# Token stage in 64-row parts on column tiles, W products summed by the back product, odd keys reversed by copy, and a new order

## The chip, the core and the metric

The kernel runs on one core of a Trainium2 chip. A core has engines that work side by side and meet by semaphores: TensorE (PE: matmuls; its weight loads are listed as PEld), VectorE (DVE), ScalarE (ACT) and GpSimd (POOL). SyncE (SP) issues nearly all transfers to 16 DMA engines. The metric is device time in microseconds of one execution; the profile's span runs from the first to the last instruction of one profiled execution.

## The reference

x has 2048 tokens of D = 640 features; there are 32 heads of 20 features and four segments of 512 tokens.

```python
x = A_x
g = sigmoid((x * gate_w).sum(-1))
a = _A_ref(x, wq, wk, wv, wo, beta)     # attention with memory
b = _B_ref(x, w_r, w_i)                 # spectral filter
return g * a + (1 - g) * b

# A, per segment s: q, k, v = x @ wq, x @ wk, x @ wv
logits = q @ k.T * scale + mask         # causal inside the segment
a_dot = softmax(logits) @ v
a_mem = (phi(q) @ M) / (phi(q) @ z + 1e-6)      # phi(t) = t + 1 if t > 0 else exp(t)
o = sigmoid(beta) * a_mem + (1 - sigmoid(beta)) * a_dot
M, z = M + phi(k).T @ v, z + phi(k).sum()
a = o @ wo

# B
X = rfft2(x)                            # over 2048 tokens and 640 features
b = irfft2(X * (w_r + 1j * w_i)).astype(bfloat16)
```

## The kernel before

**Order.** The program records operations with what they read and write (`Sched.op`), then `schedule` takes a list of numbers, `ORDER`, that fixes for each engine which operation comes when, and on which engine an operation with a choice runs. The wait instructions follow from the reads and writes (`emit`). A PSUM bank is given out by `place` inside `schedule`: banks 0 to 3 in one piece for scores, banks 4 to 7 one by one for the rest. Every engine works its list strictly in order; SP's list is the order in which transfers are issued.

**Attention.** `proj_tile` makes q and k transposed (features on partitions, 512 tokens as columns) with x transposed (xT) streaming; keys of every second 128-token tile are taken with their two 64-token halves swapped (`token_order`). ACT or DVE copies the result to `qu`, it goes to DRAM (`qk_scr`) and comes back as padded heads (`qkp`, 20 of 32 rows used). `qk_unit` forms scores in three kinds of units (whole 512-column pieces, 128-row pieces, and a last kind for two head groups at once), ACT takes the exponential of a whole unit (L1265) into `ex`, and POOL zeroes what the causal mask forbids (`mask`, L1286, 7 instructions per group of 4 heads). `pv_flipped` (segments 0 to 2) and `pv_group` (segment 3) multiply by the values `va`; the sums go to `ub` and to DRAM (`u_scr`). `v_part` projects the values; tiles with swapped halves are made by two 64-wide matmuls that stand side by side in PE's columns. `mem_update` and `mem_read` hold the memory.

**Spectral part (`fft`).** The tokens are split as 128 x 16. First `fold` forms sums and differences over features on DVE and POOL (L902, L907). F1 is the transform over the 128 (`fcat`). Then come 16 groups g, each of 128 rows: D (`big`,`Ac`) transforms the features, one product for the cosines and one for the sines, with 641 columns each in three matmuls; the results are copied to `Bt`. T (`Bt`,`tt`) finishes the tokens: two matmuls of 321 columns, over the cosine and over the sine part, for each of the real and imaginary outputs. W_mul (L1441) multiplies each with w_r and w_i at once into `Pt`; two W_add (L1446, on DVE or POOL) form real and imaginary part `Yt`. The back product Tb (`tt`,`Yt`) makes three chunks of 256 columns from both parts, and its copy goes to `Cp`. After all groups, Db (`big`,`Cp`) transforms the features back (16 steps, two types, three chunks of 128, 128 and 65 rows), and L1487 sums the halves into `G`.

**End.** `finish_tile` adds, in one PSUM bank, the gated spectral rows (`G`,`fbg`) and the projection with wo (`wo`,`oU`, L513, split by 32 columns; for segment 3 `wo`,`oTl`), copies to `ot` and writes out.

In the profile almost all matmuls have the line of the helper `mms`, L515 (L513 where a matmul is split by 32 columns), and copies from PSUM those of `copy_alts`, L524 (ACT) and L526 (DVE); so go by the names.

Of the kernel before, what the change touches and what calls it, by code (L numbers as in the profile page):

```python
# [20 lines left out]
VW = 22  # L21

# [22 lines left out]
class Op:  # L45
    __slots__ = ("id", "alts", "preds", "succs", "prio", "banks", "nbytes", "npred", "eng", "t0", "t1",
                 "stamp", "need_inc", "dyn", "first", "outside", "name", "dma", "key", "xfer", "lock", "mode", "emode", "hold", "width")


class Sched:  # L50
    HOP = 70.0
# [8 lines left out]
    def op(self, alts, r=(), w=(), prio=0.0, nbytes=0, name="", after=(), dma=False, xfer=0.0, lock=False, mode=0, hold=False, width=16):  # L60
# [24 lines left out]
        for b in w2:  # L85
            bb = b
            if isinstance(b, Bank):
                o.banks.append(b)
                b.ops.append(o)
                bb = b.buf  # L90
            dep(bb.w)
            for q in bb.r:
                dep(q)
# [10 lines left out]
        if name in ("gate_tab", "den_gate") and not o.banks:  # L104
# [4 lines left out]
    COST = {(0, 1): 94.0, (0, 2): 94.0, (1, 0): 110.0, (1, 2): 110.0, (2, 0): 110.0, (2, 1): 94.0,  # L109
            (0, 4): 105.0, (1, 4): 105.0, (2, 4): 105.0, (4, 0): 105.0, (4, 1): 105.0, (4, 2): 105.0}  # L110

    def schedule(self, pools, order, nsem=56):


        ops = self.ops
        queue = {e: [] for e in self.eng}
        for v in order:
            o = ops[v // 2]
            o.eng = list(o.alts)[v % 2]
            queue[o.eng].append(o)  # L120
        for o in ops:
            o.dyn, o.t1 = [], None
            o.first = [b for b in o.banks if b.ops[0] is o]
            for b in o.banks:
                b.left = len(b.ops)
        pe, held = queue["pe"], {}
        for i, o in enumerate(pe):
            o.emode = o.mode
            if o.mode < 0:
                modes = [held[id(b)] for b in o.banks if id(b) in held]  # L130
                if not modes and i and pe[i - 1].emode not in (1, 4):
                    modes = [pe[i - 1].emode]
                for q in pe[i + 1:] if not modes else ():
                    m = q.mode if q.mode >= 0 else held.get(id(q.banks[0]), -1)
                    if m >= 0:
                        modes = [0 if m == 1 else m]
                        break
                o.emode = (modes + [0])[0]
            if o.emode not in (1, 4):
                for b in o.banks:  # L140
                    held[id(b)] = o.emode
        pos = {e: 0 for e in self.eng}
        free = {e: 0.0 for e in self.eng}
        port = mode = 0
        level = {k: {q: 0.0 for q in v} for k, v in pools.items()}
        users = {}
        ring = [0.0] * 16
        sems = [[0.0, i, None] for i in range(nsem)]
        issued = []
        self.order = []  # L150

        def place(b, lev):
            best = None
            for pool in b.pools:
                v = lev[pool]
                for q in v:
                    run = [v.get(q + i) for i in range(b.n)]
                    if None not in run and (best is None or max(run) < best[0] - 1e-9):
                        best = (max(run), pool, q)
            return best  # L160

        def window():
            tot, i = 0, len(issued) - 1
            while i >= 0 and tot <= self.WINDOW:
                tot += issued[i].nbytes
                i -= 1
            return issued[i] if i >= 0 else None

        def head(e):
            if pos[e] == len(queue[e]):  # L170
                return None
            o = queue[e][pos[e]]
            t = free[e]
            for p in o.preds:
                if p.t1 is None:
                    return None
                if p.eng != "pe" or e != "pe":
                    t = max(t, p.t1 + self.HOP)
            if o.first:
                lev = {k: dict(v) for k, v in level.items()}  # L180
                for b in o.first:
                    got = place(b, lev)
                    if got is None:
                        return None
                    t = max(t, got[0])
                    for i in range(b.n):
                        lev[got[1]][got[2] + i] = None
            if o.dma:
                gate = window()
                if gate is not None:  # L190
                    t = max(t, gate.t1 + self.HOP)
            if e == "dve" and o.lock:
                t = max(t, free["pool"])
            elif e == "pool":
                t = max(t, port)
            return t

        while len(self.order) < len(order):
            best = None
            for e in self.eng:  # L200
                t = head(e)
                if t is not None and (best is None or t < best[0] - 1e-9):
                    best = (t, e)
            if best is None:
                raise RuntimeError("order cannot be kept: " + str([(e, queue[e][pos[e]].name, queue[e][pos[e]].id) for e in self.eng if pos[e] < len(queue[e])]))
            t, e = best
            o = queue[e][pos[e]]
            pos[e] += 1
            for b in o.first:
                _, b.pool, b.bank = place(b, level)  # L210
                for q in range(b.bank, b.bank + b.n):
                    level[b.pool][q] = None
                    o.dyn.extend(users.get(q, ()))
            o.t0 = t
            occ, lat = o.alts[e][1:]
            if e == "pe" and o.emode != mode:
                occ += self.COST[mode, o.emode]
                mode = o.emode
            free[e] = o.t1 = t + occ
            if e == "dve" and o.lock:  # L220
                port = t + occ
            if o.dma:
                if o.hold:
                    free[e] = max(free[e], max(ring) + 170.0)
                for q in range(o.width):
                    ring[q] = max(ring[q], free[e] + 1300.0) + o.xfer
                o.t1 = max(ring[:o.width])
                free[e] += 43.0
                gate = window()
                if gate is not None:  # L230
                    o.dyn.append(gate)
                issued.append(o)
                sems.sort(key=lambda q: (q[0], q[1]))
                sm = sems[0]
                if sm[2] is not None:
                    o.dyn.append(sm[2])
                sm[0], sm[2] = o.t1, o
                o.stamp = sm[1]
            o.t1 += lat
            self.order.append(o)  # L240
            for b in o.banks:
                b.left -= 1
                if b.left == 0:
                    for q in range(b.bank, b.bank + b.n):
                        users[q] = list(b.ops)
                        level[b.pool][q] = max(p.t1 for p in b.ops) + self.HOP
        self.makespan = max(o.t1 for o in ops)
# [215 lines left out]
class Kern:  # L463
# [342 lines left out]
    def record(self):  # L806
# [4 lines left out]
        for s in range(NSEG):  # L811
            self.project(s)
            if s > 0:
                self.mem_read(s)
# [794 lines left out]
```

## Time and profile before

| | us |
|---|---|
| Median of three runs (range) | 242.41 (241.71 to 244.06) |
| Span of the profiled execution | 239.9 |
| ACT exponentials L1265, 92 instructions | 138.7 |
| POOL masks L1286, 224 instructions | 121.3 |
| DVE W_mul L1441, 32 x 0.822 | 25.6 |
| W_add L1446, 16 on POOL, 16 on DVE | 11.7 and 5.5 |

The profile gives for each group of like instructions the summed busy time, the mean of one and the idle time ahead of them on their engine with what ended it. Instructions of one engine can overlap at their edges, so busy time counts the union. A matmul's time includes a tail in which the next one already streams; the distance from start to start is the better price. The DMA engines moved 42.1 MB; their mean busy share is above 0.9 in several slices of the first third. The granted TensorE clock is 1.00 throughout.

### The profile page before, as it was taken

What the parts mean: (1) busy time and instruction counts of PE and PEld (TensorE: products, weight loads), DVE (VectorE), ACT (ScalarE), POOL (GpSimd) and SP (SyncE); (2) the same over time, 40 slices, a digit from 0 to 9 for tenths busy, and PEclk for the clock granted to TensorE, in tenths of its full rate; (3) what the DMA queues carried; (4) which work ended last, traced back from release to release, by engine and by line L of the source; (5) the groups of instructions that cost most, each with busy time, mean ns of one, the idle gap of its engine ahead of it and who ended that gap; (6) DMA issues with size and microseconds to landing.
All of it is one profiled execution on the core that took longest, in us unless ns stands there. A gap on an engine that the chain in (4) does not pass through costs nothing.

```text
span 239.9 us, 9221 instructions
## 1 busy us (share of the span) xinstructions
PE 225.7 (94%) x3837; PEld 138.7 (58%) x3849; DVE 195.9 (82%) x481; ACT 199.1 (83%) x241; POOL 165.8 (69%) x297
## 2 busy tenths in 40 slices
PE   7899999999999999999989999899999998998994
PEld 2475567765456566455646555455544456665793
DVE  0479998889899996898999798997988887855563
ACT  2189688898899999999999979999999987896730
POOL 8514259457969956937974999875899867686820
PEclk9999999999999999999999999999999999999999
DMA  7999869984996795473788672364766698992223
GB/s 157 270 369 234 228 177 182 311 156 112 209 263 161 128 240 170 106 240 76 239 221 251 159 222 65 103 168 138 193 193 187 202 220 127 100 110 80 61 85 109
DMA packets 58924, 42.11 MB, mean 176 GB/s; under 512 B 30020, under 2 KB 55172, under 8 KB 58884
## 3 DMA queue, kind: packets, MB, share of 16 engines
q1 hardware_dynamic: 57844, 40.96, 70.2%
q8 instruction: 30, 0.49, 0.9%
q10 hardware_dynamic: 1040, 0.57, 0.8%
q14 instruction: 10, 0.08, 0.1%
HBM read 23.32 MB, written 12.30 MB: 148 GB/s over the span
## 4 chain that ended last, share of the span: by engine, by line
PE 57%; DVE 17%; ACT 15%; DMA 4%; issue 3%; SPq 2%; POOL 0%; DVEq 0%; ACTq 0%
PE psum L515 51%; ACT ex L1265 10%; PE psum L513 6%; DVE Pt L1441 3%; DMA out_dram<-ot 2%; DMA wk<-in_A_wk_dram 2%; SPq L547 2%; DVE xsb L907 2%; DVE xf L902 2%; ACT et L1073 1%; DVE va L1116 1%; DVE ub L526 1%; DVE phk L1086 1%; DVE q L526 1%; DVE phk L1085 1%
## 5 line engine op out<-in xcount | busy, mean ns | idle before, releaser
L1265 ACT ACTIVATE ex<-psum 128x2048 bf16<-128x2048 f32 (+4 forms) x92 | 138.7, 1507 | 12.6 <-PE psum L515 11.2
L1286 POOL TENSOR_SCALAR_AFFINE_SELECT ex<-ex 128x256 bf16<-128x256 bf16 (+2 forms) x224 | 121.3, 563 | 39.0 <-ACT ex L1265 35.6
L515 PE MATMUL psum<-xT,wk 128*128 128x256 bf16 (+1 forms) x280 | 34.0, 273 | 1.0 <-DMA wk<-in_A_wk_dram 0.8
L515 PE MATMUL psum<-qkp 20*64 20x64 bf16 (+5 forms) x1024 | 31.5, 266 | 3.4 <-ACT ex L1265 2.4
L515 PE MATMUL psum<-wv,xT 128*64 128x320 bf16 (+3 forms) x240 | 30.1, 303 | 0.4 <-DVE va L1116 0.3
L515 PE MATMUL psum<-xT,wq 128*128 128x512 bf16 (+1 forms) x123 | 27.1, 380 | 0.8 <-DMA xT<-in_A_x_dram 0.5
L1441 DVE TENSOR_TENSOR Pt<-psum,Wt 128x642 bf16<-128x642 f32 x32 | 25.6, 822 | 2.3 <-PE psum L515 1.9
L515 PEld LDWEIGHTS psum<-xT,wk 128*128 128x128 bf16 (+1 forms) x280 | 19.9, 97 | 7.5 <-DMA wk<-in_A_wk_dram 1.1
L515 PEld LDWEIGHTS psum<-qkp 20*64 20x64 bf16 (+1 forms) x1024 | 12.2, 100 | 20.4 <-ACT ex L1265 14.4
L513 PE MATMUL psum<-wo,oU 128*32 128x320 bf16 x480 | 21.9, 300 | 0.0
L907 POOL TENSOR_TENSOR xsb<-xf 128x320 bf16<-128x320 bf16 (+2 forms) x12 | 9.4, 787 | 16.6 <-DVE xsb L907 12.4
L515 PEld LDWEIGHTS psum<-wv,xT 128*64 128x64 bf16 (+1 forms) x240 | 14.9, 105 | 7.7 <-issue 2.6
L1116 DVE TENSOR_TENSOR va<-psum,ebx 128x320 bf16<-128x320 f32 x32 | 15.2, 483 | 4.4 <-ACT gate L1114 2.3
L515 PE MATMUL psum<-big,Ac 128*128 128x160 bf16 (+2 forms) x96 | 18.1, 258 | 0.7 <-DVE Pt L1441 0.3
L515 PE MATMUL psum<-big,Cp 128*128 128x321 bf16 (+1 forms) x96 | 18.1, 303 | 0.2 <-DVE G L1487 0.2
L515 PE MATMUL psum<-ex,va 128*32 128x512 bf16 (+4 forms) x480 | 17.3, 275 | 0.9 <-DVE Pt L1441 0.3
L1487 DVE TENSOR_TENSOR G<-eo,psum 128x320 bf16<-128x320 f32 x32 | 14.7, 482 | 3.5 <-PE psum L515 2.5
L526 DVE CAST ot<-psum 128x320 bf16<-128x320 f32 x21 | 10.0, 490 | 8.7 <-PE psum L513 5.3
L515 PE MATMUL psum<-tt,Yt 128*128 128x256 bf16 (+1 forms) x96 | 16.5, 275 | 0.3
L515 PEld LDWEIGHTS psum<-ex,va 128*32 128x32 bf16 x480 | 10.4, 96 | 9.9 <-POOL ex L1286 3.3
L1073 ACT ACTIVATE et<-qu 128x512 bf16<-128x512 bf16 x25 | 15.6, 629 | 0.2
L513 PEld LDWEIGHTS psum<-wo,oU 128*32 128x32 bf16 x480 | 12.0, 96 | 4.6 <-issue 1.2
(99 smaller groups left out, 391.1 us busy)
## 6 DMA issues: line engine op xcount, KB each, us to landing
qkp<-qk_scr SPq DMA_DIRECT2D x28, 160.0 KB
tt<-tab_tt SPq DMA_DIRECT2D x8, 512.0 KB, 3.9
qk_scr<-qu SPq DMA_DIRECT2D x12, 256.0 KB, 3.5
u_scr<-ub SPq DMA_DIRECT2D x12, 256.0 KB, 4.0
xsb<-in_A_x_dram SPq DMA_DIRECT2D x8, 320.0 KB, 6.4
oU<-u_scr SPq DMA_DIRECT2D x15, 128.0 KB, 3.1
out_dram<-ot SPq DMA_DIRECT2D x12, 160.0 KB
Wt<-in_B_w_r_dram SPq DMA_DIRECT2D x16, 80.2 KB, 3.4
```

The costliest lines, as they stand in the source:

```text
L513: h = e.matmul(dst, wt, r_, start=st, stop=sp_, **{**kw, "tile_position": (0, q), "skip_group_check": True})
L515: h = e.matmul(o_, l_, r_, start=st, stop=sp_, **kw)
L526: alts["dve"] = (lambda e: e.tensor_copy(dst(), src()), 67 + 1.04 * n, 68.0)
L547: return e.dma_start_transpose(d_, s_)
L902: self.either(lambda e, r=r, op=op: e.tensor_tensor(xf.ap(r * 642, [321, 2], [1, 320]), xs.ap(o, [D, 2], [1, 320]), xs.ap(o + 320, [D, 2], ...
L907: self.either(lambda e, dst=dst, src=src, d0=d0, n=n, op=op: e.tensor_tensor(xs.ap(o + dst, [D, 2], [1, n]), xf.ap(src + d0, [321, 2], [1, ...
L1073: self.one("act", lambda e: e.activation(et.ap(0, [1, L]), qsl(), ACT.Exp), L, [qb], [b("et", pi_)], late, name="phi_exp")
L1116: self.one("dve", lambda e: e.tensor_tensor(va.ap(i * H * VW + h0 * VW, [VW, nh], [1, DH]), self.ps(bank, 0, [DH, nh], [1, DH]), self.ebx. ...
L1265: self.one("act", lambda e, d=d, q=q: e.activation(self.ex.ap(*d), self.ps(bank, *q), ACT.Exp, scale=SC), n, [bank], [self.exb(s, 2 * pr + ...
L1286: self.one("pool", lambda e: e.affine_select(self.ex.ap(e0 + d0, [1280, 4], [1, n], np_=np_), self.ex.ap(e0 + s0, [1280, 4], [1, n], np_=np_),
L1441: self.one("dve", lambda e, ri=ri, Pt=Pt, Wt=Wt, wo_=wo_, bank=bank: e.tensor_tensor(Pt.ap(ri * 322, [644, 2], [1, KD]), self.ps(bank, 0, ...
L1487: self.one("dve", lambda e, q=q, n2=n2, bank=bank, eo=eo: e.tensor_tensor(self.G.ap(n2 * D + 639 * q, [1 - 2 * q, 320]), eo.ap(q, [1, 320] ...
```

## The change

The token stage works in 32 parts of 64 rows instead of 16 groups of 128. The two products of D go to the lower and the upper half of PE's columns, so that one bank holds 64 cosine rows over 64 sine rows (`mode=-2` lets D run as 64-wide tiles). T is then one matmul of 321 columns per part, its 128 output rows being 64 real over 64 imaginary. W_mul multiplies these by w_r and w_i at once, with W in 128 rows in which each row stands twice; the two W_add are left out, because the back product takes the w_r product and the w_i product with two different tables and sums them in PSUM. Its chunks are 107 rows each (KN), and so are those of `Cp` and Db.

W comes in this row order by way of DRAM: 20 transfers reorder w_r and w_i into a scratch (`w_scr`), and 8 loads bring it in, each row to two partitions.

Keys of odd tiles are taken wholly reversed instead of with swapped halves, and values likewise: `xR`, a reversed copy of the odd tiles of xT made once per segment on POOL or ACT, is the weight operand of one 128-wide matmul instead of two 64-wide ones. The gate's column for these tiles, which must not be reversed, is a matmul of one column. The masks fit the reversed order and cover fewer elements; the last kind does two groups in one instruction where their places in `ex` follow each other.

`schedule` no longer hands out banks or computes times: the lists `ORDER`, `HOMES` (banks), `TILED` (which operations run as column tiles) and `ENDED` are written out and new, and an engine no longer waits for itself where two of its operations merely share a bank (`ordered`).

```diff
-            for typ in range(2):
-                bank = Bank(1, "gen")
-                parts = ((0, 160, 161, 0), (1, 0, KD, 162), (2, 0, 160, 484)) if typ == 0 else (
-                    (2, 0, 160, 644), (3, 0, KD, 804), (4, 160, 161, 1126))
...
+            for half in range(2):
+                for n_, parts in enumerate((((0, 160, 161, 0), (2, 0, 160, 644)), ((1, 0, KD, 162), (3, 0, KD, 804)), ((2, 0, 160, 484), (4, 160, 161, 1126)))):
+                    for typ, (c, c0, n, tc) in enumerate(parts):
+                        def th(...):
+                            return (self.ps(bank, c0, [1, n], p0=64 * typ, np_=64), self.Ac.ap(c * 2048 + half * 1024 + g * 64, [1, 64]), big.ap(tc, [1, n]),
+                                    n_ == 0, n_ == 2, {"skip_group_check": True})
+                    self.mms(items, ..., name="D", mode=-2)
...
-            for ri in range(2):
-                for q in range(2):
-                        return (self.ps(bank, 0, [1, KD]), tt.ap(to + (2 * ri + q) * P, [1, P]), Bt.ap(q * 322, [1, KD]), q == 0, q == 1, {})
+                    return (self.ps(bank, 0, [1, KD]), tt.ap(to, [1, P]), Bt.ap(0, [1, KD]), True, True, {})
...
-            for r, (a0, a1, op) in enumerate(((0, 3, ALU.subtract), (1, 2, ALU.add))):
-                self.either(fn, KD, [Pb[0][r], Pb[1][1 - r]], [Yb[r]], prio2, ..., name="W_add")
...
+                for c in range(3):
+                    for x in range(2):
+                            return (self.ps(bank, c * P, [1, P], np_=KN), Pt.ap(x * 322 + c * KN, [1, KN]), tt.ap(to + P + x * P, [1, P]), x == 0, x == 1, {})
...
+    def reorder_w(self, prio):
+        for late in range(2):
+            for r, wd in enumerate((self.wr_d, self.wi_d)):
+                for half in range(2):
+                    for h in range(2):
...
+                            self.dma(lambda: dap(self.Wd.ap(), ...), lambda: dap(wd, so, *src), ..., name="mv_W" + str(late))
...
-        return [(0, 256, lambda: xT.ap(c * L, [256, 2], [1, P])), (256, 256, lambda: xT.ap(c * L + P + 64, [256, 2], [-64, 2], [1, 64]))]
+        return [(0, 256, lambda: xT.ap(c * L, [256, 2], [1, P])), (256, 256, lambda: xT.ap(c * L + 2 * P - 1, [256, 2], [-1, P]))]
...
+        rev = lambda: (xR.ap(0, [256, 5], [P, 2], [1, P]), xT.ap(2 * P - 1, [L, 5], [256, 2], [-1, P]))
+        self.Sc.op({"pool": (lambda e: e.tensor_copy(*rev()), 1340.0, 50.0), "act": ...}, r=xb, w=[b("xR", s)], name="xrev", ...)
...
-            for p0, t0, n in ((0, 64, 64), (64, 0, 64)) if i % 2 else ((0, 0, P),):
-                items.append((lambda ...: (self.ps(bank, 0, [1, w], p0=p0, np_=n), xT.ap(c * L + i * P + t0, [1, n]), ...
+            items = [((lambda c=c: (self.ps(bank, 0, [1, w]), xR.ap(c * 256 + (i // 2) * P, [1, P]) if i % 2 else xT.ap(c * L + i * P, [1, P]), ...
+            if h0 and i % 2:
+                items.append(((lambda c=c: (self.ps(bank, 320, [1, 1]), xT.ap(c * L + i * P, [1, P]), ...
...
+    @staticmethod
+    def ordered(p, o):
+        return p.eng == o.eng and not p.dma and (p.eng == "pe" or p in o.preds and p.id not in o.hard)
```

## The prediction

> **What bounds the kernel now.** I read the page's first two parts, then the engine times in five stretches, the chain of waits, the groups by form, and the waits of the weight loads. The stretches are cut where the ninth long exponential starts (52.3 us), the 53rd (189.0 us) and where the last matmul ends (236.5 us); a long one is an ACT instruction at L1265 of 2048 or 1280 elements, 64 in all.
>
> ```profile
> PE 225.7 (94%) x3837; PEld 138.7 (58%) x3849; DVE 195.9 (82%) x481; ACT 199.1 (83%) x241; POOL 165.8 (69%) x297
> ...
> 0.00:12.00 12.00, 9.34 (x130) 4.31 (x131) 2.90 (x7) 2.31 (x4) 8.81 (x13) 1.00 0.93 213
> 12.00:52.30 40.30, 39.67 (x485) 26.58 (x488) 36.07 (x88) 34.51 (x54) 19.34 (x34) 1.00 1.00 245
> 52.30:189.00 136.70, 130.84 (x1954) 75.25 (x1963) 124.57 (x310) 128.68 (x144) 106.62 (x198) 1.00 0.66 172
> 189.00:236.50 47.50, 45.85 (x1272) 32.55 (x1270) 31.87 (x78) 33.62 (x41) 31.05 (x54) 1.00 0.63 120
> ```
>
> The columns of a stretch are its length, then PE, weight loads, DVE, ACT and POOL, then clock, DMA share and GB/s. In the long middle stretch ACT works 128.7 of 136.7 us. PE's 130.8 looks busier, but a matmul's time holds a tail that the next one overlaps, so I price PE by the distance of starts:
>
> ```profile
> 122.24 0.44 PE L515 MATMUL psum<-Bt,tt 128*128 128x321 bf16 x2
> 20.21 0.87 PE L515 MATMUL psum<-wv,xT 128*64 128x320 bf16 x10
> 123.39 0.84 PE L515 MATMUL psum<-tt,Yt 128*65 128x256 bf16 x6
> ```
>
> One 321-column matmul lasts 0.302 us and two take 0.44, so a second costs 0.138. Ten 64-wide ones last 0.304 each and take 0.87: four further pairs in 0.57, 0.14 a pair, so two share the time of one. Six 256-column ones cost (0.84 - 0.27) / 5 = 0.114 each, less inside a run. Columns thus cost 0.42 ns each, in pairs of 64-wide tiles half that. A change of tile shape costs PE about 0.094 us beyond the stream: from 20 value matmuls 32 wide at 121.13 to the 128-wide one at 121.79 is such a step: those 20 end 0.73 later, the last lasts 0.22 (128 columns), so it starts at 121.64, and the next one 0.15 after it instead of the 0.054 of its stream. Priced so, with 232 changes of shape in program order (21.8 us), PE's own work is 214 us, of which 123.3 lie between the two exponentials, 13 less than the stretch. There ACT is the tighter engine. The waits agree:
>
> ```profile
> PEld psum L515 <- ACT ex L1265: 14.4, 46, 0.7
> PEld psum L515 <- POOL ex L1286: 4.3, 14, 0.5
> PEld psum L515 <- DVE Pt L1441: 3.8, 15, 0.6
> ```
>
> The chain of waits is PE for 57% of the span, DVE 17%, ACT 15%: at most places PE is late by its own work, and most often it is ACT that holds it up.
>
> **The change, part by part.** The instruction order of the changed kernel gives all counts.
>
> Token stage. The forward product T goes from 64 to 32 matmuls of 321 columns: 32 x 0.138 = -4.4 us of PE. The D product goes from 96 matmuls to 96 pairs over the same columns, so 0 to first order. The back product keeps its 24,576 columns (96 x 256 before, 192 x 128 after): 0. The 32 W_add go: 16 x 0.365 on DVE (5.5 us) and 16 x 0.732 on POOL (11.7). W_mul stays at 32 x 0.822. A short D pair streams 160 columns, 0.069 us, while its two weight loads last 0.105 each by the row of 64-wide loads (0.097 for 128-wide ones). If both had to end in that time, 64 short pairs would cost up to 0.036 x 64 = 2.3 us; at the least nothing, or a little below if two shorter loads hide better than one. I take nothing, because the scores' 64-wide loads start 0.003 apart and overlap. The Trainium skill, TensorEngine Tiling (Array Packing), "Feature Incompatibilities", speaks against the change here: column tiling excludes the fast weight load. With 64 columns at 1.2 a nanosecond (the Trainium skill, TensorE: Matmul & The Clock Gate, "LDWEIGHTS"), two loads in a row take an estimated 107 ns against the 69, so the sum would be 2.4 us worse. The 105 against 97 in the trace agrees only faintly, and no row shows a short pair.
>
> Changes of tile shape: 232 become 237, +0.5 in all, but 159 become 175 in the middle, +1.5, while start and end lose 4 and 7.
>
> Odd keys. The 80 pairs of the value projection become 80 matmuls 128 wide, at 0.136 the same. 40 one-column matmuls for the gate come on top; 320 score-times-value matmuls of 21 columns stand 0.025 apart, so +1.0. The copies xR are 4 on POOL of 1280 elements: a 2832-element memset takes 2.46 (so 1.1), a 640-element sum of two sources 1.40 (so 2.8). I take 1.4 each, nearer the memset because there is one source: 5.6 us of POOL; its cover is POOL's third of idle time, and without it each would hold five value matmuls and the masks queued behind it. 100 key matmuls and 40 tiled ones now read 128 columns backwards where they read two runs of 64. No row has PE reading backwards. DVE does at L907 (353 ns for 320 elements, against 365 for the 321 of Yt, all forwards), so at the low end nothing; at the high end the scattered weights of the last projection, 139 against 96 ns, a ratio of 1.45: 100 x 0.049 + 10 x 0.049 = +5.4. I take nothing: the step of one element is the fold's, not the 16 of those weights.
>
> Masks on POOL: 128 + 64 + 32 of 0.478, 0.670 and 0.691 us (124.3) become 126 of 256 elements and 65 of 512 (105.0): -19.3. With W_add -11.7, the copies +5.6 and some 9.6 of sums and scalings moved over from DVE, POOL loses 16 us.
>
> ACT and DVE. ACT's list between the two exponentials loses 7 Bt copies (0.538 each), has 7 Cp copies of 384 elements (0.485, midway between 0.368 and 0.602) for 6 of 256 and 6 of 512, 4 fewer gate exponentials (0.165), one qu and one eo fewer, and gains 6 ub copies (0.608) and an ot: -3.8 - 2.4 - 0.7 - 0.6 - 0.4 + 3.6 + 0.4 = -3.9 us. DVE takes 8 Bt (4.2), the larger share of Cp (+2.9) and Ac (+2.7) and loses the 5.5 of W_add, 7 ub (4.8), 3 ot (1.5) and 6.2 of small work that goes to POOL; with 1.8 of eo and folds, -6.4. It was 124.6 of 136.7 busy in the middle, so this is cover and no path. Waits of an engine for itself fall from 27 to 10 on ACT, 133 to 99 on DVE, 99 to 55 on POOL; a gain that no row prices, at least 0; I leave it out.
>
> W by way of DRAM. The 32 loads of 82 KB (2.63 MB) become 20 moves of the same bytes inside DRAM and 8 loads of 657 KB (5.26 MB); the tables shrink by 1.05 MB. Net +4.2 MB on 42.1. By the time the first new W load is issued, 12 moves and that load stand in SP's queue, some 1.9 MB for 0.4 MB before (1.4 more, with the smaller table), in a stretch where the DMA share is 1.00 at 245 GB/s. The big table, pad loads, key transposes and the third x load are queued behind some of them, and D, T and the scores wait for these. Uncovered, 1.4 MB is 5.7 us. I cost it at nothing, for PE has the projections of the second segment and the first transform to do; issue slots fall too, 232 to 228 on SP.
>
> **The sum.** In the middle ACT sets the length: -3.9 us, PE's own -1.5 lying under it. In the start PE sheds 4 shape changes and some D and state products that move later: -0.5. In the end, 7 shape changes and three groups of the projection, against three back products more: -0.7. Together -5.1. The profiled span is 239.9, so 234.8 after; the median of the runs, 242.4, is 2.5 above the span, and with that **237.3 us**.
>
> **The rivals.**
> 1. The gaps close as well. ACT idles 8.0 us of the middle, PE waits 4.3 for masks and 1.4 for W_add sums; masks get shorter and W_add vanishes. If half of the 8.0 goes, 233.3 us. For it: all four engines carry less, 3 to 10%. Against it: most waits are for ACT, whose exponentials (138.7 us) stay.
> 2. The relief is hidden. If the middle is set by the hand-over between scores, exponential and PSUM bank, the copies that ACT loses ran in cover; only PE's -2.9 (-4.4 + 1.0 + 0.5) counts, and a new order may give some of it back: 240 to 242 us. A slow backward read (+5.4) ends here too, at 242.7. For it: ACT waits 11.2 us for PE; against it: from 145 to 158 us ACT's list shows no gap.
> 3. The DMA queues become the bound of the first third, and the kernel is slower. The moves run ahead of the big table and of the pads. The place is the stretch from 12 to 52 us, and the second group of eight moves (1.4 MB) stands before the next W load: 5.7 + 5.7 us of queue. Beyond 7.5 us not covered by projections the result is over 1% slower; all of it gives 242.4 + 11.4 - 5.1 = 248.7, the likely share about 246. For it: the share of 1.00. Against it: 349 GB/s from 10 to 20 us shows room, and after 52 us the share is 0.66.
>
> **The numbers.** Forecast 0.47 (234.5 to 239.5), rival 1 0.25, rival 2 0.16, rival 3 0.12. A change of 1%, 2.4 us, is what this measurement can tell from none: below 240.0 lie the forecast and rival 1, faster 0.71; rival 2 and the mildest of 3 give the same, 0.17; slower 0.12. The range reaches from well into rival 1 to the edge of rival 3: 231 to 244.5.
>
> **What would show it.** T at 32 matmuls 0.138 apart and no Yt; D pairs 0.003 apart with steps of 0.07 and 0.14; backward key matmuls at 0.109; ACT near 125 us between the same two exponentials, with the middle at about 133; masks near 105 us. It is wrong if the first exponentials come later than before with the weight loads waiting for DMA (rival 3), or if ACT's gaps in the middle grow by what its work shrinks (rival 2).

## The result and the profile after

The changed kernel takes 325.69 us, the median of four runs (321.52 to 327.78), against 242.06 for the kernel before on the same chip. Some executions of a kernel here take a few per cent longer than its others, and the ratios, here 1.330 with a 95% interval of 1.321 to 1.339, leave out those more than 1.5% above its fastest. The forecast was 237.3, the range ended at 244.5, and the one rival on the slow side ended at 248.7: the time lies far outside all of them.

The engines hardly work more than before; they stand. These are the page's busy times and its chain of waits for the changed kernel:

```profile
span 325.9 us, 9399 instructions
...
PE 247.0 (76%) x3969; PEld 153.0 (47%) x3969; DVE 198.4 (61%) x464; ACT 194.7 (60%) x223; POOL 142.1 (44%) x263
...
PEclk9999979959956959769859995978958999969999
...
PE 40%; DMA 36%; SPq 8%; DVE 8%; ACT 4%; issue 2%; POOL 1%; DVEq 0%; ACTq 0%; POOLq 0%
```

Before, PE was 57% of that chain, DVE 17% and ACT 15%. Now transfers are 36%. DVE and ACT carry what they carried (195.9 and 199.1 us then), POOL 24 us less, and PE's 21 us more come with a lower clock: the mean granted clock is 0.87, and nearly all slices with a 5 or a 6 lie in or right behind those in which PE is least busy.

The stretches of the prediction, cut at the ninth and the 53rd long exponential (56.9 and 272.9 us) and at the last matmul; the columns are as in the prediction:

```profile
0.00:12.00 12.00, 8.16 (x118) 3.91 (x122) 1.77 (x5) 1.88 (x2) 6.06 (x10) 1.00 0.88 209
12.00:56.90 44.90, 40.70 (x478) 27.14 (x471) 36.31 (x89) 32.50 (x47) 21.18 (x33) 0.96 1.22 228
56.90:272.90 216.00, 150.10 (x2122) 88.02 (x2123) 129.78 (x298) 126.77 (x132) 84.20 (x170) 0.83 0.59 128
272.90:322.70 49.80, 48.05 (x1263) 33.96 (x1261) 30.00 (x74) 33.57 (x43) 30.62 (x51) 0.93 0.52 113
```

The middle went from 136.7 to 216.0 us, 79 of the 86 us by which the span grew. In it the DMA share fell from 0.66 to 0.59. Transfers hold the kernel up while two fifths of the engines' time for them is free, so it is not their amount. Who waits there, from the view of waits (engine, line, what it waits for, us, times, longest):

```profile
ACT ex L1328 <- PE psum L451: 73.9, 36, 13.1
...
DVE Pt L1504 <- DMA Wt<-w_scr: 32.5, 4, 10.5
...
PE psum L451 <- DMA tt<-tab_tt: 9.9, 2, 5.6
```

And the six longest transfers of the chain, in order of time (start, length, what):

```profile
81.38 16.58 DMA Wt<-w_scr
...
102.34 16.59 DMA pkn<-phk
...
120.42 17.18 DMA qk_scr<-qu
...
184.60 12.53 DMA tt<-tab_tt
...
203.54 13.66 DMA tt<-tab_tt
...
223.01 16.02 DMA Wt<-w_scr
```

They make 92.6 us of chain. Two are loads of W. The others are transfers that the change did not make slower: a transpose of keys, a store of queries, the tables. All have about the same length, which suggests one thing that they all stand behind. The packet records show it. For each of the 8 W loads (642 KB in 128 packets of 5136 bytes) I took the time from its first packet's start to its last one's end, and the sum of its packets' times over that; beside them some loads of tt (256 packets of 1536 bytes), where the last 32 come late:

```
W load at    lasts     mean packets in flight
 53.2 us     13.19 us   2.0
 82.8        14.49      2.0
102.8        13.26      2.0
120.8        14.84      2.0
180.4        14.31      2.0
199.3        14.92      1.9      (the other two: 13.7 and 13.9 us, 2.0 and 1.9)

tt load at  94.2:  224 packets in 2.54 us, the last 32 from 99.8 on
tt load at 185.6:  224 packets in 2.17 us, the last 32 from 194.5 on
```

A W load has two packets on the way, where 16 engines could carry one each. The transpose waits from 102.34 to 118.93 us while a W load lasts from 102.8 to 116.0, the store from 120.42 while one lasts from 120.8, and both tt pieces lie over W loads too. And 32 of 256 packets are two sixteenths: in four of the eight tt loads fourteen sixteenths are there in 1.7 to 2.5 us, and two sixteenths come 3 to 8 us later; in the other four nothing comes late. So the theory before the experiments was: a W load runs on two of the 16 DMA engines, for 13 to 15 us, and of every transfer issued meanwhile the part that falls to these two waits behind it. The source of the load begins with `[0, 2]`, the two copies of 64 rows. That number two is the suspect. The Trainium skill, DMA: Bandwidth & Descriptors, "Rules for kernel authors", states it: an outermost dimension smaller than 16, a zero-step broadcast of c copies for one, confines the whole DMA to at most c engines. The 2.0 in flight agrees.

The rivals were the added bytes (4.2 MB, my third rival in the prediction), the order that the change brings, and the reading of scratch rows just written, twice.

### The profile page after: what moved, and what is told of

The parts are those of the page before. It is cut to its first block, busy times and chain, and to the rows that moved or that the text cites. A ratio compares the mean times of both kernels' runs of the same rounds, so it can differ in the third digit from the quotient of the medians.

```text
span 325.9 us, 9399 instructions
## 1 busy us (share of the span) xinstructions
PE 247.0 (76%) x3969; PEld 153.0 (47%) x3969; DVE 198.4 (61%) x464; ACT 194.7 (60%) x223; POOL 142.1 (44%) x263
## 4 chain that ended last, share of the span: by engine, by line
PE 40%; DMA 36%; SPq 8%; DVE 8%; ACT 4%; issue 2%; POOL 1%; DVEq 0%; ACTq 0%; POOLq 0%
PE psum L451 34%; DMA Wt<-w_scr 10%; DMA qk_scr<-qu 8%; DMA tt<-tab_tt 8%; PE psum L449 6%; SPq L485 5%; DMA pkn<-phk 5%; SPq L483 3%; ACT ex L1328 3%; DMA xsb<-in_A_x_dram 2%; DMA w_scr<-in_B_w_i_dram 1%; DVE Pt L1504 1%; DMA qkp<-qk_scr 1%; DVE qu L462 1%; DVE G L1538 1%
## 5 line engine op out<-in xcount | busy, mean ns | idle before, releaser
L1354 POOL TENSOR_SCALAR_AFFINE_SELECT ex<-ex 128x256 bf16<-128x256 bf16 (+3 forms) x191 | 92.9, 506 | 121.6 <-ACT ex L1328 119.0
L1504 DVE TENSOR_TENSOR Pt<-psum,Wt 128x642 bf16<-128x642 f32 x32 | 26.1, 822 | 49.7 <-DMA Wt<-w_scr 32.5
L451 PE MATMUL psum<-wv,xT 128*128 128x1 bf16 (+2 forms) x120 | 24.3, 287 | 6.8 <-ACT qu L460 6.7
L451 PE MATMUL psum<-tt,Pt 128*107 128x128 bf16 x192 | 20.7, 253 | 11.3 <-DVE Pt L1504 10.6
L451 PE MATMUL psum<-Bt,tt 128*128 128x321 bf16 x32 | 11.1, 347 | 19.1 <-DMA tt<-tab_tt 9.9
L451 PEld LDWEIGHTS psum<-tt,Pt 128*107 128x107 bf16 x192 | 17.3, 154 | 16.1 <-DVE Pt L1504 10.9
L451 PE MATMUL psum<-wv,xR 128*128 128x320 bf16 x80 | 16.8, 318 | 6.5 <-DVE Pt L1504 6.5
L451 PE MATMUL psum<-big,Cp 107*128 107x321 bf16 x96 | 17.5, 311 | 0.8 <-DVE on L1396 0.5
L451 PEld LDWEIGHTS psum<-wv,xT 128*128 128x128 bf16 x120 | 12.0, 106 | 12.5 <-ACT qu L460 6.8
L958 POOL TENSOR_TENSOR xsb<-xf 128x322 bf16<-128x322 bf16 (+2 forms) x11 | 9.1, 838 | 19.8 <-DVE xf L953 19.8
L460 ACT ACTIVATE qu<-psum 128x512 bf16<-128x512 f32 x17 | 10.1, 594 | 11.6 <-DMA qk_scr<-qu 7.1
```

What stands on the lines that cost most here:

```text
L451: h = e.matmul(o_, l_, r_, start=st, stop=sp_, **kw)
L460: alts["act"] = (lambda e: e.activation(dst(), src(), ACT.Copy), 65 + 0.833 * n, 110.0)
L958: self.either(lambda e, dst=dst, src=src, d0=d0, n=n, op=op: e.tensor_tensor(xs.ap(o + dst, [D, 2], [1, n]), xf.ap(src + d0, [321, 2], [1, ...
L1354: self.one("pool", lambda e: e.affine_select(self.ex.ap(e0 + d0, [1280, n4], [1, n], np_=np_), self.ex.ap(e0 + s0, [1280, n4], [1, n], np_ ...
L1504: self.one("dve", lambda e, Pt=Pt, Wt=Wt, wo_=half * 2 * KD + sl * KD, bank=bank: e.tensor_tensor(Pt.ap(0, [322, 2], [1, KD]), self.ps(ban ...
```

## The experiments

Each time is the median of a kernel's runs. It stands with the ratio to runs of the kernel before on the same chip (243.0 to 243.9 us in the median) and the 95% interval of that; a time with no interval comes from a single run or from very few. Runs of one kernel spread by 2 to 11 us.

### The load without the two at its head

```diff
- dma(Wt.ap(0, [1, 8 * KD]), dap(Wd, g // 2 * 64 * 8 * KD, [0, 2], [8 * KD, 64], [1, 8 * KD]))
+ for d in range(2):   # one operation, two DMAs
+     dma(Wt.ap(0, [1, 8 * KD], p0=64 * d, np_=64), dap(Wd, g // 2 * 64 * 8 * KD, [8 * KD, 64], [1, 8 * KD]))
```

> Each W load is issued as two DMAs of 64 rows, so that neither begins with the two-step dimension; the bytes, the moves inside DRAM and the order stay. Narrow-load theory (the dimension of two at the head of the source confines a load to 2 of the 16 DMA engines, and what is queued on those two waits for it): a W load falls from the 13.2 to 14.9 us of the changed kernel to under 5, its mean of 2.0 packets in flight rises above 6, the seven waits of 10 to 17 us leave the chain, and the time is what the prediction's sum gave without the loads, 237 us, at most 243. Added-bytes theory (4.2 MB more in all, and 2.6 MB of moves ahead of the loads, fill the engines): the same bytes move, so most of the 84 us stays, over 300 us. New-order theory (the instruction order is bad, whatever the loads take): over 290 us.

258.3 us in the median of six runs (254.28 to 265.34), ratio 1.049 (1.042 to 1.057). The bytes, moves and order are the same, and 67 us are gone: in the ratio, 0.28 of the loss of 0.33. A load now lasts 2.9 to 7.5 us with 6.4 to 14.8 packets in flight. The idle time of VectorE before the W products, from the view of the tile Wt, first of the changed kernel (32.5 us of waiting for W in four waits), then of this one:

```profile
  DMA Wt<-w_scr: 32.5, 4
```

```profile
  PE psum L452: 1.6, 5
  DMA Wt<-w_scr: 0.5, 1
```

The added bytes and the order are out as the main cause. But 237 to 243 was expected, and 15 us stayed: a second cause, or several.

### A four at the head, in blocks that lie together

```diff
- dap(Wd, g // 2 * 64 * 8 * KD, [8 * KD, 64], [1, 8 * KD])
+ dap(Wd, g // 2 * 64 * 8 * KD, [16 * 8 * KD, 4], [8 * KD, 16], [1, 8 * KD])
```

> As the kernel with two DMAs of 64 rows, but each source begins with a dimension of four (four blocks of 16 rows, the same bytes in the same place). Narrow-load theory: each DMA keeps to 4 engines, so a load has 4 packets in flight, or up to 8 if its two halves take different engines, and lasts about 7 us (half of 13.2 to 14.9) or 3.5; the time lies between the kernel with halves and the changed one, 245 to 290 us at 7 us a load. A theory in which it is the row read twice, not the leading number, that is slow: no different from the halves, within 1%.

258.92 us, as the kernel with halves. The loads last 2.8 to 8.4 us with 5.7 to 15.1 in flight, so they did not keep to four engines. It looks like a miss for the theory, but the four blocks of 16 rows follow each other without a gap, and are the same access as 64 rows; I read it so that the two dimensions were joined before the transfer was cut up, which the zero step of the broadcast doesn't allow. The run tells nothing of widths, and neither does the next.

### The tables with a two at the head, in blocks that lie together

```diff
- dap(tab["tt"], g * P * TT, [TT, P], [P * TT, 2], [1, TT])
+ dap(tab["tt"], g * P * TT, [64 * TT, 2], [TT, 64], [P * TT, 2], [1, TT])
```

> The kernel with two DMAs of 64 rows for each W load, and now the 8 loads of the transform tables (tt, 384 KB each, 256 rows of 1536 bytes) have a source that begins with two (two blocks of 64 partitions); bytes and places as before. Narrow-load theory: the tt loads go from 1.2 to 2.5 us to 2 packets in flight and, by the W loads' 0.021 us a KB (13.5 us for 642 KB), about 8 us each or more, and a part of the loss comes back: 250 to 300 us. If it were something peculiar to the W loads (rows read twice, scratch): as the kernel with halves, within 1%.

262.19 us, 1.5% above the kernel with halves and inside its spread. The tt loads had 4.0 to 12.8 packets in flight, and 3.9 to 12.6 in the kernel with halves: not narrow, for the same reason. Two expectations were wrong because the edit did not make what it was meant to; the next experiment on widths uses steps that can't be joined.

### Narrow loads from the input, hardly any moves

```diff
- dap(Wd, g // 2 * 64 * 8 * KD, [0, 2], [8 * KD, 64], [1, 8 * KD])
+ dap(wr_d, 0, [0, 2], [8 * KD, 64], [1, 8 * KD])
  # and each of the 20 moves: all columns -> 16 elements a row
```

> The changed kernel with its narrow loads kept, 8 of 642 KB with two at the head of the source, but read from the input w_r as it stands, and with each of the 20 moves cut to 16 elements a row: the W factors are not the right ones, and 2.6 MB of writing and nearly as much of reading go. Narrow-load theory: the loads keep 2 packets in flight and 13 to 15 us each, and the time stays above 305 us. Added-bytes theory: with the moves go more than half of the bytes that came on top, so the time falls by at least 40 us, under 285. A theory in which the loads are slow because they read scratch just written: the loads get short, under 5 us, and the time falls to about 237 us.

325.78 us: nothing comes back. The loads take 13.1 to 15.0 us at 2.0 in flight. With the broadcast at the head neither the scratch tensor nor the 2.6 MB of moves matters; the narrow load covers all that.

### Widths measured

```diff
+ WIDE = (2, 2, 4, 4, 8, 8, 16, 16)      # k of the eight tt loads; table rows interleaved to match
- dap(tab["tt"], g * P * TT, [TT, P], [P * TT, 2], [1, TT])
+ dap(tab["tt"], g * P * TT, [2 * TT, k], [k * 2 * TT, P // k], [1, 2 * TT])
```

> A measurement of widths. The kernel with two DMAs of 64 rows for each W load; the rows of the transform table lie interleaved in DRAM, and each of the 8 loads of tt (384 KB, 3072 bytes a row) begins with a dimension of 2, 2, 4, 4, 8, 8, 16, 16 that can't be merged with the next, since its step is the smaller one; no row is read twice. Narrow-load theory: mean packets in flight near 2, 4, 8 and up to 16, the load lasting about 8 us, 4, 2 and 1.2 to 2.5; time above the kernel with halves by up to 8 us, for the first two loads. If only the reading of rows twice makes a load narrow: all eight at 8 to 14 in flight and 1.2 to 4 us.

From the packet records of the eight loads (384 KB, 128 packets of 3072 bytes each):

```
k at the head        2      2      4      4      8      8     16     16
lasts, us          9.59   8.31   7.57   5.25   3.32   3.44   3.50   1.64
packets in flight   2.0    1.9    4.0    3.9    6.9    6.8    9.1   12.4
```

The number at the head of the source sets how many packets are on the way, 2, 4, nearly 8, and more at 16; nothing is read twice here. The length does not go quite as its inverse, for a packet takes 0.125 to 0.249 us in the mean of a load, longest in the third load and the first one of 16, where other transfers ran beside it. The time was 270.97 us: six loads of 8 that keep to 2, 4 or 8 engines cost 13 us over the median of the kernel with halves, in a single run.

### Narrow loads alone, in the old order

```diff
# the kernel before; its tt table interleaved by rows of pairs
- dap(tab["tt"], g * P * 1024, [1024, P], [P * 1024, 2], [1, 1024])
+ dap(tab["tt"], g * P * 1024, [2048, 2], [4096, 64], [1, 2048])
```

> The kernel before, with one thing alone: its 8 loads of transform tables (512 KB each) get a source that begins with a dimension of two (rows interleaved in the DRAM table, 4096 bytes a row, the same bytes). Narrow-load theory: by the 0.022 us a KB of the first narrow loads (8.3 to 9.6 us for 384 KB) each takes 11 to 13 us at 2 packets in flight, other DMAs stand behind them, and the kernel loses at least 15 us, 258 to 310 us, without any move, broadcast or new order. Order theory: a kernel whose order is not the new one rides it out: within 2%.

314.89 us against 242.95. Nothing of the change is in this kernel, only that its 8 table loads of 512 KB begin with a two; the bytes are the same. Each takes 10.8 to 12.0 us with 2.0 in flight. Its chain has the pieces that the changed kernel had, again not only of the load itself:

```profile
86.30 11.93 DMA pkn<-phk
...
125.71 13.46 DMA tt<-tab_tt
...
147.82 13.39 DMA tt<-tab_tt
...
169.40 13.03 DMA qk_scr<-qu
...
189.19 13.81 DMA tt<-tab_tt
...
211.83 12.60 DMA tt<-tab_tt
```

So narrow loads are enough by themselves to lose 72 us, in a single run; the new order isn't needed for it.

### The moves

```diff
# halves_nomove: on the kernel with halves; all eight loads read the same 64 rows
- 20 moves of w_r and w_i to w_scr
- dap(Wd, g // 2 * 64 * 8 * KD, [8 * KD, 64], ...), waits for the moves
+ dap(wr_d, 0, [8 * KD, 64], ...), no wait
# halves_input: all moves kept, loads from wr_d, no wait
# moves_small: as halves_input, each move 16 elements a row
```

> The kernel with each W load as two DMAs of 64 rows (258.3 us), with the 20 moves inside DRAM left out and the loads taken from the input w_r as it stands, without a wait for moves: the W factors are not the right ones; all the rest is computed. Moves theory (the 20 moves, 2.6 MB each way, take queue and engines in the first 80 us, and the loads wait for them behind SP's order): the start shift of 4.6 us at the fourth long exponential shrinks to under 1.5, the step of 4 us between the 13th and the 16th goes, and the time falls by 6 to 9 us to about 250. Order theory (the late x loads, the held VectorE instructions and the waits belong to the new order): no more than 2 us come back, 256 or above.

249.42 us (247.69 to 255.30), ratio 1.019 (1.010 to 1.028): 9 us by the medians and 7 by the ratios, as the moves theory said. The step from the 13th to the 16th long exponential is smaller (they come 0.9 and 1.8 us later than before, not 3.8 and 7.7), but the fourth is still 4.5 us late: that part of the expectation failed, and its lateness is not the moves' doing.

> The kernel with two DMAs of 64 rows, with all 20 moves kept, but the W loads read w_r as it stands and do not wait for the moves (the W factors are not the right ones). It parts the moves' 8.9 us. If it is the wait (SP stands at the first W load until the moves have landed, and all DMAs behind it stand too, 7 us at 65 us): most of it comes back, 250 to 252. If it is the moves' place in SP's queue and their time on the engines: no more than 2 us, 256 or above.

261.74 us, ratio 1.070 (1.061 to 1.080), worse than with the wait. The wait is not the price; that what it holds back would otherwise meet the moves on the engines is a guess.

> The kernel with two DMAs of 64 rows whose loads read w_r as it stands and wait for no move (261.7 us with whole moves, 249.4 with none): all 20 moves are issued in their places, but each carries 16 elements a row, about 40 KB in all instead of 2.6 MB (the W factors are not the right ones). Traffic theory (the moves' time on the engines, when their share is at 1.00, delays what is behind them): most of the 12 us comes back, 249 to 252. Slot theory (20 more issues of about 0.6 us stand in SP's order, 12 us of SP): 257 or above.

256.61 us (252.89 to 257.95), between the two theories. (The moves carry 20 KB in all here, not the 40 of the expectation.) Taking the traffic away gives some 5 us, taking the slots as well 7 more; with a spread of 5 us the halves of it are no better known than that. The slots are seen in the chain of the kernel with halves, where eight moves are issued in a row while SP is what everyone waits for:

```profile
60.39 0.62 SPq L488
...
61.05 0.63 SPq L488
...
65.42 6.99 DMA w_scr<-in_B_w_i_dram
...
73.03 5.26 DMA Wt<-w_scr
```

### Held VectorE instructions

The kernel with halves has VectorE instructions that last far longer than their kind. From the views of the tiles phq (phi of the queries) and oU (the attention sums, multiplied by r), minimum, median and maximum in ns; first the kernel before, then the one with halves:

```profile
L1086 DVE TENSOR_TENSOR phq<-phq,et x15: 404/416/615, 39.1 to 162.4; 128x512 bf16<-128x512 bf16 x15
L1528 DVE TENSOR_TENSOR oU<-oU,r x13: 361/419/870, 173.1 to 203.5; 128x512 bf16<-128x512 bf16 x13
```

```profile
L1149 DVE TENSOR_TENSOR phq<-phq,et x15: 415/425/3464, 37.4 to 174.5; 128x512 bf16<-128x512 bf16 x15
L1604 DVE TENSOR_TENSOR oU<-oU,r x10: 400/416/3853, 193.5 to 221.6; 128x512 bf16<-128x512 bf16 x10
```

While the one of 3853 ns lasts, POOL runs four products end to end (1158, 1142, 1143 and 1138 ns, the first from before it), and VectorE goes on when the run ends; the one of 3464 ns lies under masks and a copy xR. PE stands 2.9 us (195.2 to 198.1) and 2.7 us (137.3 to 140.0) beside them. In the kernel before no VectorE instruction lasts over 1.3 us. The Trainium skill, SBUF — State Buffer, "SBUF: two separate sides", has the two engines share a port pair under an exclusive lock that the loser waits for; these rows agree, and one instruction here waited for a whole run. Is that the rest of the loss?

```diff
# halves_xR_act, on the kernel with halves: xR copies POOL -> ACT
# halves_both: that, and no moves (as halves_nomove)
# halves_port: halves_xR_act, and all products and sums on oU POOL -> DVE
# nomove_port: that, and no moves
```

> The kernel with two DMAs of 64 rows for each W load, and the four copies xR on ACT instead of POOL; W and moves as they were. Held-port theory (a VectorE instruction that meets a run of POOL work is held, 3.46 us for a phq minimum that takes 0.50 elsewhere, 1.68 for a maximum that takes 0.28, both while the 1.24 us copy xR runs): these two long instructions go, no other VectorE instruction over 2 us appears but the oU products, and the time falls by 2 to 4 us. Rival (the held instructions are covered, since VectorE has room): the time stays within 1%; by the length of the copies on ACT, 4 of about 1.1 us, it could even rise by up to 4 us.

253.79 us (252.69 to 254.76), ratio 1.042 (1.035 to 1.048), against 1.049 (1.042 to 1.057): the intervals overlap. The phq instruction is still held, but for 2.27 us instead of 3.46: the 1.19 us less are the length of the copy that left POOL (1.24).

> Both edits on the kernel with two DMAs of 64 rows: no moves (W factors from w_r as it stands, not the right ones), and the xR copies on ACT. If moves and held port are two causes that add, the time falls by the sum of the two single falls, to 246 to 250 us, 1 to 3% over the kernel before; if the order loses the rest whatever these two do, it stays above 254.

250.49 us, ratio 1.020 (1.010 to 1.030): as without the xR edit (1.019). They do not add.

> The kernel with two DMAs of 64 rows and the xR copies on ACT, and now all oU products and sums on VectorE (5 products and 4 sums were on POOL); moves and W as they are in the changed kernel. Held-port theory (a VectorE product that meets a run of POOL work is held, 3.85 and 2.13 us for oU where 0.42 is usual, and PE stands 3.1 to 3.3 us at one of them): no oU product over 1 us, and the time falls by 3 to 5 us from the 253.8 of the kernel with xR on ACT, to 249 to 251. Rival (they are held in cover, or VectorE's longer list gives it back): within 1% of 253.8.

255.68 us, ratio 1.046 (1.038 to 1.055): no gain. The longest oU product lasts 2.14 us.

> The same with the 20 moves left out and the W loads taken from w_r as it stands (the W factors are not the right ones). Held-port theory: 250.5 less 3 to 5 us, 245 to 247.5, 1 to 2% over the kernel before. If it came to 239 or less, the three causes (narrow loads, moves, held port) would make up the whole miss against the predicted 237.3; at 245 some 8 us of it lie in the new order or in terms of the sum that were wrong, PE's above all.

251.62 us (247.18 to 252.19), no gain either. In its trace a gap of 2.5 us of PE that ends at 148.0 us, with no releaser, has come where none was. Going by the times, these four are misses for the held-port theory as the rest of the loss.

But the edits did not remove the holds. The phq product is held in all four (2.27 us), and one oU product too (2.1 us, and in halves_both another of 3.85). And the trace of the kernel without moves, from its timeline, shows a hold on the path: the copy Bt stands behind the phq product on VectorE, PE waits for the copy and ACT for PE.

```profile
128.37 3.46 DVE L1149 TENSOR_TENSOR phq<-phq,et 128x512 bf16<-128x512 bf16 x1
131.76 0.51 DVE L463 CAST Bt<-psum 128x322 bf16<-128x322 f32 x1
...
132.32 0.35 PE L452 MATMUL psum<-Mz,phq 128*128 128x88 bf16 x3 [2.65 <-DVE Bt L463]
...
133.05 1.88 ACT L1331 ACTIVATE ex<-psum 128x2048 bf16<-128x2048 f32 x1 [2.85 <-PE psum L452]
```

With that the long exponentials, 0.2 us early at the 32nd against the kernel before, are 2.8 us late at the 33rd. The held oU product of 3.86 us, with PE idle for 3.1, takes them from 2.1 us at the 50th to 5.0 at the 51st. These two steps are 6 us, and at the 53rd the kernel is 6.3 us late in all. In halves_both the first step is 1.8 us instead of 3.0, by as much less as the phq product is held less; a saving of 1.2 us is too small to be seen in these times. One more try cut POOL's work in both kernels:

```diff
# masks that work in place, in both kernels
- affine_select(ex[.., n columns a head])
+ affine_select(ex[.., 4 columns a head])
```

> The kernel before with its masks in place cut from 64 or 128 columns a head to 4 (the causal masking of the scores is left out there; the masks that also copy stay whole). POOL loses about two thirds of its 124 us of masks. It is the base for the next kernel. Held-port theory: no VectorE instruction is held long in the kernel before, so little comes back: the 4.3 us for which PE waits for masks at most, 238 to 243 us.

242.13 us, ratio 0.994 (0.990 to 0.999).

> The same cut of the masks in the kernel with two DMAs of 64 rows and no moves (249.4 us; W factors not the right ones, masking left out in place). Held-port theory (VectorE instructions stand behind POOL's runs, and PE behind them: 2.8, 3.3, 1.4 and 0.9 us in that kernel's trace): with POOL nearly empty the long ones go but for that behind POOL's oU products and the xR copy, and the time falls by 4 to 7 us more than the kernel before falls by the same edit. Rival (the 6 us over the kernel before lie in PE's own work and the new order): it falls by as much as the kernel before, and the two stay 5 to 7 us apart.

246.06 us, ratio 1.011 (1.006 to 1.016). The kernel without moves falls from 1.019 to 1.011, the one before from 1 to 0.994, so the two stay 1.65% apart where they were 1.9%: about 4 us. A net gain from short masks is thus not shown, though the intervals leave room for one of up to some 3 us. And a hold is left on the path: the phq product at 37.4 us lasts 3.48 us under short masks, folds and a copy xR, and PE stands behind it:

```profile
41.59 0.62 PE L452 MATMUL psum<-fcat,xsb 128*128 128x128 bf16 x8 [2.35 <-DVE Ac L463]
```

This last kernel's profiled execution has a granted clock of 0.999 and shows the change without its narrow loads and its moves best. Its fourth long exponential comes 4.6 us later than before, the ninth 3.0, the last one 1.9. The middle:

```profile
56.10:192.30 136.20, 130.83 (x2122) 79.49 (x2122) 120.59 (x297) 126.13 (x133) 57.24 (x169) 1.00 0.80 186
```

The line's stretch begins and ends 0.8 us behind the starts of the two exponentials; from start to start it is 136.2 us too. That compares with 136.0 in the kernel before with short masks (136.7 with whole ones). With whole masks and no moves the middle is 142.3. In none of them did it become shorter.

## Why the prediction was wrong

**The step that failed: W by way of DRAM, costed at nothing.** I counted bytes, 657 KB a load, against what all DMA engines move, and asked whether 1.4 MB more in a queue could stay covered. The price is not by bytes over 16 engines. A load with a two at its head takes 13.2 to 14.9 us with two packets in flight, and transfers behind it make pieces of 12.5 to 17.2 us in the chain. Eight of them made 67 of the 84 us. The source pattern with `[0, 2]` was there to read in the changed kernel.

**Rival 3 had the side and neither the size nor the place.** It put the loss between 12 and 52 us and at most at 11.4 us. There it is 4.6 us (the ninth exponential at 56.9 instead of 52.3), and in the middle, where I had read a DMA share of 0.66 as room, it is 79. A mean share says nothing of the two engines that a load is confined to. The moves, which that rival did price (their bytes and place in SP's queue), cost 7 to 9 us, part slots and part traffic: "issue slots fall too" was true of the count and not of the place, eight in a row ahead of a W load.

**PE's terms.** Distances from start to start, stalls and changes of shape left out, in the last kernel above against the kernel before: T 4.48 us against 9.20, so -4.7 (predicted -4.4). The 40 one-column matmuls 1.18 (+1.0). D 9.82 against 9.68: +0.1 (0 taken). The rule of the Trainium skill, TensorEngine Tiling (Array Packing), "Feature Incompatibilities", that column tiling excludes the fast weight load, would by the prediction's estimate have made it 2.4 us worse; no run shows that. The key matmuls read backwards: 22.16 against 22.53, nothing (0 taken; the end of 5.4 was far off). The back product was mis-sized: 11.93 us against 7.51 + 3.75 = 11.26, +0.7 (0 taken). The five further changes of shape (+0.5 taken) no run prices apart. Most terms held, but PE's own time came out about level, where the sum of its terms was -2.9: all distances under 0.4 us sum to 213.5 us before and 215.0 in the last kernel, those under 0.5 us to 222.2 and 222.8. So 3 to 4 us more went into groups of matmuls that neither the prediction nor this list prices; which they are stays open.

**ACT sets the middle: the mechanism failed too.** ACT's work there went from 128.7 to 126.8 us in the changed kernel (126.1 in the last one), not by the 3.9 predicted but by 1.9 to 2.6. And where neither loads nor moves disturb it and the masks are short, the stretch keeps its 136 us: ACT's gaps grew by what its work shrank (10.1 us of gaps against 8.0 before), which the prediction had named as the sign of rival 2. So without the loads and moves I would now expect the 240 to 242 of rival 2 at best; no run here has the right W without either, so this is not shown.

**Masks and VectorE.** The masks came to 95.7 us on POOL against 105.0 predicted, since those of 256 elements took 0.42 us and not 0.48. That VectorE falls by 6.4 in the middle was wrong in the changed kernel (129.8 against 124.6): held instructions count as busy. With short masks it is 120.6, against 122.8 in the kernel before with short masks.

**Open.** The fourth long exponential comes 3.9 to 5.4 us late in every kernel with the new order. That is mostly the new order itself: the third starts at 20.70 us in the last kernel and at 20.72 before, and between the two ACT's list now has eight instructions where it had two, some 3 us more, and ACT waits 1.6 us for PE. At the ninth the three kernels without moves and with whole masks are only 0.0 to 0.7 us late. What the change loses without its narrow loads and moves lies behind that: in the traces of halves_nomove and of the last kernel for the most part at held VectorE instructions, in that of nomove_port also at the gap without a releaser. But no run of the new order is without holds, so what the time would be without them is not shown, and neither is how much of the last 4 us they make.

## What to carry to other kernels

Read each DMA's access patterns before its bytes: the outermost number, where it can't be joined with the next, capped the packets in flight here (2, 4, under 8, and 9 to 12 at 16), and a long narrow load delays whatever is queued behind it. To copy rows to two halves of the partitions, issue two DMAs with the rows outermost rather than one with a broadcast ahead. A DMA share of 0.6 is no sign of room when transfers of one length stand in the chain; count the packets in flight.

## What the runs showed of the hardware

That a narrow load stops others was worse than its own length suggests: with 224 of 256 packets of a table there in 1.7 to 2.5 us, the whole transfer waited 3 to 8 us for the last 32, in four loads of eight.

PE's granted clock fell with the waits: a mean of 1.00 before, 0.87 in the changed kernel, 0.89 in the kernel before with narrow table loads. The 2122 matmuls of the middle were busy for 150.1 us in the changed kernel, at a clock of 0.83 there, and for 130.8 in the last kernel of the experiments, at 1.00, which adds to what the waits themselves cost.

A VectorE product that usually takes 0.42 us lasted 3.85 us beside a run of four POOL products of 1.14 to 1.16 us, and PE and ACT stood behind such holds for 2.4 to 3.1 us at a time.
